# Spreading part of one weight matrix over few DMA engines and reordering the head and tail of a fused GQA-and-MLP decode kernel

## The chip, the cores and the metric

The kernel runs on one core of one Trainium2 chip. The metric is the device time of one execution in microseconds (us); the time before is the median of three runs, 681.97 us (681.95 to 682.03). A core has five engines (PE for matmuls, DVE for vector work, ACT for activations, POOL, and SP, which here only issues transfers) and sixteen DMA engines that bring data from main memory (HBM) into the on-chip memory (SBUF, 128 partitions).

## What is computed

One decode step of a block for 8 sequences: attention over a cache of 4096 positions (32 query heads that share 8 key/value heads in groups of 4), times a gate from a small gated MLP, plus the input.

```python
xn = _layernorm(x)                                  # 8 x 512
q  = xn @ wq                                        # 512 x 4096 weights
p  = softmax(q k^T * Dh**-0.5)                      # k_cache: 8 x 8 x 4096 x 128
s  = (p v) @ wo                                     # wo: 4096 x 512
z  = gelu(xn @ w_in);  z1, z2 = split(z);  z2 = _layernorm(z2)
g  = silu((z1 * (w_sp * z2 + b_sp)) @ w_out)        # w_out: 896 x 512
out = x + s * g
```

All data are 32-bit floats. The two caches are 134 MB each, so nearly all of the 291 MB that the kernel moves is read once and used once.

## The kernel before

**Loads.** Everything that comes from HBM goes through a ring of three SBUF slots of 16384 floats per partition (`ring`, `bufs=3`); a transfer into a slot is issued from SP's queue when the slot's last user is done. The order on SP is: one transfer `w_mlp` (L59: `w_in`, `w_out` and a small `side` block, 10880 floats per partition), `wq` (L74), and then for each of the 8 key/value heads two halves of K (`load_k`, L288) and two halves of V (`load_v`, L295). The input `x` (8 rows of 2 KB) is loaded from ACT's queue (L71). The last half of V comes in two pieces, with the output weights `wo` around it: blocks 0 to 7 ahead of it (L318) and blocks 8 to 31 behind it in nine pieces of falling size (`WO_PIECES`, L321), the last four of one block each (128 rows of 2 KB). A transfer over 128 partitions is shared by all sixteen DMA engines, eight rows each.

**Order of the work.** The head normalises `x` (L122 to L130), runs `mlp()` (L145 to L201, which leaves the gate in `gate`), then `project_q` twice (L208 to L220, which fills `qz`). Per head: `scores` for two halves (L231), `softmax` (L236 to L259), `values` for two halves (L273 to L278) and `combine` (L283). PE takes its instructions in the order in which the program writes them. Temporaries of `mlp()` lie in the unused end of the MLP's slot (`from_slot`), so that slot is free only when the last of them has been read.

**The tail.** The attention output of a head is split in 4 blocks of 128 rows, 32 blocks in all, and each has to be multiplied by its 128 x 512 block of `wo`. The first `FOLDED = 29` blocks go through `project_o` (L303): block `m` is accumulated over 512 columns in strip `m % 4` of PE (the array is used in four strips of 32 columns side by side) of the PSUM tile `part`. `part` is copied to SBUF by DVE (L342), and eight small matmuls (L358) add its four strips and two column halves into `acc`. The last three blocks go `direct` (L350): eight matmuls of 64 columns for each block put it straight into `acc`. The order on PE at the end is: blocks up to 28 folded, block 29 direct (`AHEAD = 30`), the eight matmuls of L358, blocks 30 and 31 direct, and then DVE multiplies by the gate (L362), adds `x` (L363), and ACT's queue stores (L364).

Of the kernel before, what the change touches and what calls it, by code (L numbers as in the profile page):

```python
# [8 lines left out]
F32 = mybir.dt.float32  # L9
# [4 lines left out]
P = 128  # L14
B, D = 8, 512
HKV, REP, S, DH = 8, 4, 4096, 128
NK = D // P
G = 4
J = S // (G * P)
R = 32  # L20
FH = 896
FQ = 256
NB = FH // P
EPS = 1e-5
GELU_C = 0.7978845608028654
HALF = B // 2
# [2 lines left out]
W = 64  # L29
OUT_ROWS = 2 * B  # L30
WO_EARLY = 8
WO_PIECES = [(8, 14), (14, 19), (19, 23), (23, 26), (26, 28), (28, 29), (29, 30), (30, 31), (31, 32)]
FOLDED = HKV * REP - 3
AHEAD = FOLDED + 1


@with_exitstack
def tile_gqa_gmlp_decode(ctx: ExitStack, tc: tile.TileContext, x, kT, v, wq, wo, w_mlp, out, gate, stored):
    nc = tc.nc
    head = ctx.enter_context(tc.tile_pool(name="head", bufs=1))  # L40
    l = head.tile([P, HKV], F32, name="l")
# [4 lines left out]
    const = ctx.enter_context(tc.tile_pool(name="const", bufs=1))  # L46
    work = ctx.enter_context(tc.tile_pool(name="work", bufs=1))
# [4 lines left out]
    def slot():  # L52
        return ring.tile([P, SLOT], F32, name="slot")


    mlp_slot = slot()
    n_in, n_out = NK * 2 * FH, NB * D
    n_mlp = n_in + n_out + P
    nc.sync.dma_start(mlp_slot[:, :n_mlp], w_mlp)  # L59
    w_in_sb = mlp_slot[:, :n_in].rearrange("p (k n) -> p k n", k=NK)  # L60
    w_out_sb = mlp_slot[:, n_in:n_in + n_out].rearrange("p (j d) -> p j d", j=NB)
    side_sb = mlp_slot[:, n_in + n_out:n_mlp]
    spare = [n_mlp]

    def from_slot(rows, n):
        lo = spare[0]
        spare[0] = lo + n
        return mlp_slot[:rows, lo:lo + n]

    x_sb = from_slot(B, D)  # L70
    nc.scalar.dma_start(x_sb, x)  # L71

    wq_sb = slot()
    nc.sync.dma_start(wq_sb, wq)  # L74
    wq_sb = wq_sb.rearrange("p (k n) -> p k n", k=NK)


    ident = const.tile([P, P], F32, name="ident")
# [44 lines left out]
    nc.vector.bn_aggr(mv, st)  # L123
    nc.vector.tensor_scalar(rstd[:, 0:1], mv[:, 1:2], EPS, None, op0=ALU.add)
    nc.gpsimd.tensor_tensor(rstd[:, 1:2], rstd[:, 0:1], neg_half[:B, 0:1], op=ALU.pow)
# [8 lines left out]
    def mlp():  # L134
        z = from_slot(P, 2 * FQ).rearrange("p (a f) -> p a f", a=2)
        u = from_slot(P, 2 * FQ).rearrange("p (a f) -> p a f", a=2)
        pz = scratch([P, 2 * FQ], "pz")
        nc.vector.memset(pz, 0.0)
        pz_v = pz.rearrange("p (a f) -> p a f", a=2)
        w_in_v = w_in_sb.rearrange("p k (a f) -> p k a f", a=2)  # L140
        for k in range(NK):
            for g in range(G):
                lo = g * FQ
                n = min(FQ, FH - lo)
                nc.tensor.matmul(pz_v[R * g:R * (g + 1), :, :n], xnT[:, k, :],  # L145
                                 w_in_v[:, k, :, lo:lo + n], start=(k == 0), stop=(k == NK - 1))
        zf, uf = z.rearrange("p a f -> p (a f)"), u.rearrange("p a f -> p (a f)")
        nc.vector.tensor_copy(zf, pz)
        nc.vector.tensor_mul(uf, zf, zf)
        nc.vector.tensor_scalar(uf, uf, 0.044715, 1.0, op0=ALU.mult, op1=ALU.add)  # L150
        nc.vector.tensor_mul(uf, uf, zf)
        nc.scalar.activation(uf, uf, AF.Tanh, scale=GELU_C)
        nc.vector.tensor_scalar(uf, uf, 1.0, 0.5, op0=ALU.add, op1=ALU.mult)
        nc.vector.tensor_mul(zf, uf, zf)

        def mean(src, name):
            part_sum = small.tile([P, 1], F32, name="part_sum")
            nc.vector.tensor_reduce(part_sum, src, op=ALU.add, axis=AX.X)  # L158
# [12 lines left out]
        nc.vector.tensor_scalar(var, var, EPS, None, op0=ALU.add)  # L171
        rs = small.tile([P, 1], F32, name="rs")
        nc.gpsimd.tensor_tensor(rs, var, neg_half, op=ALU.pow)
        nc.vector.tensor_scalar(z2, z2, rs, None, op0=ALU.mult)
        nc.vector.tensor_scalar(z2, z2, side_sb[:, W:W + 1], side_sb[:, W + 1:W + 2],
                                op0=ALU.mult, op1=ALU.add)
        nc.vector.tensor_mul(u[:, 1, :], z2, z1)
        hT = from_slot(P, 2 * P).rearrange("p (a s) -> p a s", a=2)
        for a in range(2):
            th = scratch([P, P], "th")  # L180
            nc.tensor.transpose(th, u[:, 1, a * P:(a + 1) * P], ident)
            nc.vector.tensor_copy(hT[:, a, :], th)  # L182
        pw = scratch([P, D], "pw")
        for j in range(NB):
            g, a = divmod(j, 2)
            nc.tensor.matmul(pw[R * g:R * (g + 1), :], hT[:, a, R * g:R * (g + 1)], w_out_sb[:, j, :],  # L186
                             start=(a == 0), stop=(a == 1 or j == NB - 1))
        y_sb = from_slot(P, D)
        nc.vector.tensor_copy(y_sb, pw)  # L189
        py = scratch([P, W], "py")  # L190
        for g in range(G):
            for a in range(2):
                nc.tensor.matmul(py[R * g:R * (g + 1), :], pick[:, a, :],
                                 y_sb[:, (2 * g + a) * W:(2 * g + a + 1) * W], start=(a == 0), stop=(a == 1))
        nc.vector.tensor_copy(x_out, side_sb[:, :W])
        e = from_slot(P, W)
        nc.vector.tensor_scalar(e, py, -1.0, 87.0, op0=ALU.mult, op1=ALU.min)
        nc.scalar.activation(e, e, AF.Exp)
        nc.vector.tensor_scalar(e, e, 1.0, None, op0=ALU.add)
        nc.vector.reciprocal(e, e)  # L200
        nc.vector.tensor_mul(gate, py, e)  # L201
# [17 lines left out]
                o = b * R + b * REP  # L219
                nc.vector.tensor_copy(qz[:, h, o:o + REP], tv[:, :, g, b])  # L220

    oT = const.tile([P, HKV, REP, B], F32, name="oT")
    oT_last = const.tile([P, REP, 2, OUT_ROWS], F32, name="oT_last")
    nc.gpsimd.memset(oT_last, 0.0)

# [72 lines left out]
    part = sc[:, 0, :]  # L298

    def project_o(lo, hi):  # L300
        for m in range(lo, hi):
            h, r = divmod(m, REP)
            nc.tensor.matmul(part[R * r:R * r + B, :], oT[:, h, r, :], wo_sb[:, m, :],  # L303
                             start=(m < REP), stop=(m >= FOLDED - REP))

    mlp()
    project_q(0)
    project_q(1)
    for h in range(HKV):
        for half in range(2):  # L310
            scores(h, half, load_k(h, half))
        pT = softmax(h)
        po = po_ps[:, h % 2]
        for half in range(2):
            last = h == HKV - 1 and half == 1
            if last:
                wo_slot = slot()
                nc.sync.dma_start(wo_slot[:, :WO_EARLY * D], wo[:, :WO_EARLY * D])  # L318
                v_sb = load_v(h, half, 2)
                for lo, hi in WO_PIECES:  # L320
                    nc.sync.dma_start(wo_slot[:, lo * D:hi * D], wo[:, lo * D:hi * D])  # L321
                wo_sb = wo_slot.rearrange("p (m d) -> p m d", d=D)
                project_o(0, WO_EARLY)
            else:
                v_sb = load_v(h, half, 1)
            n = 2 if last else HALF
            for i in range(0, HALF, n):
                done = values(half * HALF + i, n, pT, v_sb[:, i:i + n])
                if half or i:
                    combine(*o_prev, po)  # L330
                o_prev = done
        combine(*o_prev, po)
        po_t = po.rearrange("p (b r) -> p r b", r=REP)
        n = min(REP, FOLDED - h * REP)
        nc.vector.tensor_copy(oT[:, h, :n], po_t[:, :n])
        if n < REP:
            for a in range(2):
                nc.vector.tensor_copy(oT_last[:, n:, a, a * B:(a + 1) * B], po_t[:, n:])

    project_o(WO_EARLY, FOLDED)  # L340
    part_sb = work.tile([P, G, DH], F32, name="o_all")
# [11 lines left out]

    direct(FOLDED, AHEAD)
    for a in range(2):
        for g in range(G):
            c = (2 * g + a) * W
            nc.tensor.matmul(acc[R * g:R * g + OUT_ROWS, :], pick[:, a, :OUT_ROWS], part_f[:, c:c + W],  # L358
                             start=False, stop=False)
    direct(AHEAD, HKV * REP)  # L360

# [42 lines left out]
```

## Time and profile before

| what | value |
|---|---|
| median of 3 runs | 681.97 us (681.95 to 682.03) |
| the profiled execution's own time | 681.93 us |
| its span, first to last instruction | 680.4 us |
| DMA, mean rate over the span | 428 GB/s |
| PE busy / PE weight loads busy | 343.5 us (50%) / 91.9 us (14%) |
| DVE / ACT / POOL busy | 87.2 / 13.4 / 3.9 us |

The profile gives, for one execution, the busy time of each engine, the DMA engines' busy share, the chain of work that ended last, and groups of instructions with their source line. `L303` is line 303 of the kernel before; after the change the same statements stand at other lines.

### The profile page before, as it was taken

What the parts mean: (1) busy time and instruction counts of PE and PEld (TensorE: products, weight loads), DVE (VectorE), ACT (ScalarE), POOL (GpSimd) and SP (SyncE); (2) the same over time, 40 slices, a digit from 0 to 9 for tenths busy, and PEclk for the clock granted to TensorE, in tenths of its full rate; (3) what the DMA queues carried; (4) which work ended last, traced back from release to release, by engine and by line L of the source; (5) the groups of instructions that cost most, each with busy time, mean ns of one, the idle gap of its engine ahead of it and who ended that gap; (6) DMA issues with size and microseconds to landing.
All of it is one profiled execution on the core that took longest, in us unless ns stands there. A gap on an engine that the chain in (4) does not pass through costs nothing.

```text
span 680.4 us, 5199 instructions
## 1 busy us (share of the span) xinstructions
PE 343.5 (50%) x2380; PEld 91.9 (14%) x2380; DVE 87.2 (13%) x229; ACT 13.4 (2%) x27; POOL 3.9 (1%) x12
## 2 busy tenths in 40 slices
PE   0475544435555453455554444555553454555557
PEld 0121111111111110111111111111111111111111
DVE  2440011102110021102100021101101021101121
ACT  0000000000000000000000000000000000000000
POOL 1000000000000000000000000000000000000000
PEclk9786666788776667878765677787666678777689
DMA  9999999999999999999999999999999999999996
GB/s 390 432 433 432 432 432 432 432 432 443 436 439 436 439 432 429 432 432 432 432 432 432 432 439 429 443 432 432 429 432 429 432 447 432 439 432 435 417 420 273
DMA packets 6661, 291.15 MB, mean 428 GB/s; under 512 B 872, under 2 KB 872, under 8 KB 1648
## 3 DMA queue, kind: packets, MB, share of 16 engines
q1 hardware_dynamic: 6480, 290.79, 98.9%
q8 instruction: 18, 0.29, 0.2%
q10 hardware_dynamic: 160, 0.05, 0.0%
q14 instruction: 3, 0.02, 0.0%
HBM read 290.80 MB, written 0.03 MB: 427 GB/s over the span
## 4 chain that ended last, share of the span: by engine, by line
DMA 77%; PE 16%; issue 4%; another core or an unknown queue 2%; DVE 1%; POOL 0%; POOLq 0%
DMA slot<-in_v 43%; DMA slot<-in_kT 28%; PE sc L231 7%; PE o_ps L273 7%; DMA slot<-in_wo 6%; PE scr L208 1%; DMA slot<-in_x 0%; PE sc L303 0%; DVE q_sb L211 0%; PE scr L214 0%; DVE o_all L342 0%; DVE slot L189 0%; DVE st L122 0%; POOLq L398 0%
## 5 line engine op out<-in xcount | busy, mean ns | idle before, releaser
L231 PE MATMUL sc<-slot,qz 128*32 128x512 f32 x1024 | 148.9, 747 | 140.6 <-DMA slot<-in_kT 140.6
L273 PE MATMUL o_ps<-slot,pT 128*16 128x512 f32 x1024 | 149.5, 748 | 113.8 <-DMA slot<-in_v 113.8
L231 PEld LDWEIGHTS sc<-slot,qz 128*32 128x32 f32 x1024 | 38.4, 134 | 244.8 <-issue 158.8
L273 PEld LDWEIGHTS o_ps<-slot,pT 128*16 128x16 f32 x1024 | 33.3, 114 | 215.9 <-issue 154.1
L236 DVE TENSOR_REDUCE nm<-sc 128x1 f32<-128x1024 f32 x8 | 9.8, 1225 | 286.2 <-PE sc L231 286.2
L276 DVE TENSOR_TENSOR o_all<-o_ps,diag 128x512 f32<-128x512 f32 x17 | 11.8, 692 | 249.1 <-PE o_ps L273 249.1
L238 ACT ACTIVATE p<-sc,nm 128x1024 f32<-128x1024 f32 x8 | 8.9, 1113 | 577.9 <-DVE nm L236 577.9
L283 PE MATMUL po_ps<-fold,o_sb 128*128 128x16 f32 x30 | 6.3, 286 | 26.8 <-DVE o_sb L278 26.8
L278 DVE TENSOR_REDUCE o_sb<-o_all 128x128 f32<-128x512 f32 x17 | 17.8, 1047 | 0.6
L145 PE MATMUL scr<-slot,xnT 128*32 128x512 f32 (+1 forms) x32 | 5.8, 830 | 9.9 <-DMA slot<-in_w_mlp 9.9
L283 PEld LDWEIGHTS po_ps<-fold,o_sb 128*128 128x128 f32 x30 | 4.8, 199 | 40.6 <-DVE o_sb L278 40.6
L303 PE MATMUL sc<-slot,oT 128*8 128x512 f32 x58 | 9.5, 593 | 1.1 <-DMA slot<-in_wo 1.0
L259 DVE STREAM_TRANSPOSE pT<-p 128x1024 f32<-128x1024 f32 x8 | 10.0, 1246 | 0.3
L241 PE MATMUL scr<-ident,nm 128*1 128x128 f32 x8 | 2.2, 270 | 10.9 <-DVE nm L236 10.9
L208 PE MATMUL scr<-slot,xnT 128*32 128x512 f32 x64 | 7.3, 594 | 0.0
L254 PE MATMUL scr<-wl,same 128*128 128x1 f32 x16 | 3.2, 272 | 6.2 <-DVE wl L252 6.2
L257 DVE TENSOR_SCALAR p<-p,w 128x1024 f32<-128x1024 f32 x8 | 6.0, 753 | 0.3
L220 DVE COPY qz<-scr 128x4 f32<-128x4 f32 x64 | 4.6, 151 | 1.5 <-PE scr L214 1.5
L160 PE MATMUL scr<-part_sum,same 128*128 128x1 f32 x4 | 1.1, 348 | 7.0 <-DVE part_sum L158 7.0
L247 PE MATMUL scr<-ident,full 1*128 1x1 f32 x8 | 1.7, 215 | 5.1 <-DVE full L245 5.1
L186 PE MATMUL scr<-slot 128*32 128x512 f32 x14 | 3.9, 1061 | 0.2 <-DVE slot L182 0.2
L254 PEld LDWEIGHTS scr<-wl,same 128*128 128x128 f32 x16 | 2.8, 219 | 6.6 <-PE scr L247 6.6
(88 smaller groups left out, 55.9 us busy)
## 6 DMA issues: line engine op xcount, KB each, us to landing
slot<-in_v SPq DMA_DIRECT2D x2, 4096.0 KB, 30.4
slot<-in_w_mlp SPq DMA_DIRECT2D x1, 5440.0 KB, 15.5
slot<-in_wo SPq DMA_DIRECT2D x1, 2048.0 KB, 34.4
slot<-in_wo SPq DMA_DIRECT2D x1, 1536.0 KB, 38.2
slot<-in_wo SPq DMA_DIRECT2D x1, 1280.0 KB, 41.2
slot<-in_wo SPq DMA_DIRECT2D x1, 1024.0 KB, 43.1
slot<-in_wo SPq DMA_DIRECT2D x4, 256.0 KB, 18.9
slot<-in_wo SPq DMA_DIRECT2D x1, 768.0 KB
```

What stands on the lines that cost most here:

```text
L208: nc.tensor.matmul(pq[R * g:R * (g + 1), :], xnT[:, k, :], wq_sb[:, k, lo:lo + REP * DH], start=(k == 0), stop=(k == NK - 1))
L231: nc.tensor.matmul(sc[R * g:R * (g + 1), c, :], qz[:, h, b * R:(b + 1) * R], k_sb[:, i, c, g, :], start=(b == 0), stop=(b == B - 1))
L236: nc.vector.tensor_reduce(m, sc, op=ALU.max, axis=AX.XY, negate=True)
L238: nc.scalar.activation(p, sc.rearrange("p c s -> p (c s)"), AF.Exp, bias=m, accum_out=l[:, h:h + 1])
L254: nc.tensor.matmul(tot, same_all, wl, start=True, stop=True)
L257: nc.vector.tensor_scalar(p, p, w, None, op0=ALU.mult)
L259: nc.vector.transpose(pT.rearrange("p j b g r -> p j g b r"), p.rearrange("p (j g b r) -> p j g b r", j=J, g=G, b=B))
L273: nc.tensor.matmul(of[R * c:R * c + G * REP, :], pT[:, j, b0 + i], v_sb[:, i, j], start=(j < rows), stop=(j >= J - rows))
L276: nc.vector.tensor_mul(o_all, o, diag[:, :, None].to_broadcast([P, G, DH]))
L278: nc.vector.tensor_reduce(o_sb, o_all.rearrange("p g d -> p d g"), op=ALU.add, axis=AX.X)
L283: nc.tensor.matmul(po[:, b0 * REP:(b0 + n) * REP], o_sb, f.rearrange("p i r -> p (i r)"), start=True, stop=True)
L303: nc.tensor.matmul(part[R * r:R * r + B, :], oT[:, h, r, :], wo_sb[:, m, :], start=(m < REP), stop=(m >= FOLDED - REP))
```

## The change

- The head's loads are now all on SP's queue in the order `wq`, `x`, `w_mlp`, two new transfers, K; `project_q` runs ahead of `mlp()`.
- The last two of the seven 128-row blocks of `w_out` leave `w_mlp` (which shrinks from 10880 to 9856 floats per partition) and come by two transfers of their own: partitions 0 to 94 from an array of 5 groups of 19 rows, partitions 95 to 127 from an array of 3 groups of 11 rows, 4 KB a row. Each group of the source is followed by an unused row, so that the groups stay a dimension of their own.
- Two temporaries of `mlp()` (`y_sb`, `e`) move out of the MLP's slot into tiles of the pool `work`.
- `FOLDED` goes from 29 to 28, so that all of the last head goes direct; blocks 26 and 27 are folded in two halves of 256 columns, each half in a strip of its own. `AHEAD` stays 30, so blocks 28 and 29 go direct ahead of the eight matmuls that add up the strips.

```diff
+EXTRA = [(5, 19), (3, 11)]
+MOVED = 2
...
-FOLDED = HKV * REP - 3
-AHEAD = FOLDED + 1
+FOLDED = HKV * REP - REP
+AHEAD = FOLDED + 2
...
+    wq_sb = slot()
+    nc.sync.dma_start(wq_sb, wq)
     mlp_slot = slot()
...
-    nc.scalar.dma_start(x_sb, x)
-
-    wq_sb = slot()
-    nc.sync.dma_start(wq_sb, wq)
+    nc.sync.dma_start(x_sb, x)
+    nc.sync.dma_start(mlp_slot[:, :n_kept], w_mlp)
+    row = 0
+    for (k, n), src in zip(EXTRA, (w_ex0, w_ex1)):
+        nc.sync.dma_start(mlp_slot[row:row + k * n, n_kept:n_mlp], src[:, :n])
+        row += k * n
...
-        y_sb = from_slot(P, D)
+        y_sb = work.tile([P, 2 * D], F32, name="y_sb", tag="pT")[:, :D]
...
-        e = from_slot(P, W)
+        e = work.tile([P, W], F32, name="e", tag="o_all")
...
-            nc.tensor.matmul(part[R * r:R * r + B, :], oT[:, h, r, :], wo_sb[:, m, :],
-                             start=(m < REP), stop=(m >= FOLDED - REP))
-
-    mlp()
+            cuts = 2 if m >= FOLDED - 2 else 1
+            n = D // cuts
+            for i in range(cuts):
+                q = 2 * (r % 2) + i if cuts == 2 else r
+                nc.tensor.matmul(part[R * q:R * q + B, i * n:(i + 1) * n], oT[:, h, r, :],
+                                 wo_sb[:, m, i * n:(i + 1) * n], start=(m < REP), stop=(cuts == 2))
+
     project_q(0)
     project_q(1)
+    mlp()
...
+    row = 0
+    for i, (m, n) in enumerate(EXTRA):
+        e = np.zeros((m, n + 1, MOVED * D), np.float32)
+        e[:, :n] = w_out[row:row + m * n, (NB - MOVED) * D:].reshape(m, n, MOVED * D)
+        arrays[f"w_ex{i}"] = e
+        row += m * n
```

More of the change, by code (lines that the diff above doesn't have):

```diff
@@ L32, with tile_gqa_gmlp_decode @@
 WO_PIECES = [(8, 14), (14, 19), (19, 23), (23, 26), (26, 28), (28, 29), (29, 30), (30, 31), (31, 32)]
-FOLDED = HKV * REP - 3
-AHEAD = FOLDED + 1
+FOLDED = HKV * REP - REP
+AHEAD = FOLDED + 2
 @with_exitstack
-def tile_gqa_gmlp_decode(ctx: ExitStack, tc: tile.TileContext, x, kT, v, wq, wo, w_mlp, out, gate, stored):
+def tile_gqa_gmlp_decode(ctx: ExitStack, tc: tile.TileContext, x, kT, v, wq, wo, w_mlp, w_ex0, w_ex1, out, gate, stored):
     nc = tc.nc
@@ L53, in slot @@
         return ring.tile([P, SLOT], F32, name="slot")
+    wq_sb = slot()
+    nc.sync.dma_start(wq_sb, wq)
+    wq_sb = wq_sb.rearrange("p (k n) -> p k n", k=NK)
     mlp_slot = slot()
     n_in, n_out = NK * 2 * FH, NB * D
-    n_mlp = n_in + n_out + P
-    nc.sync.dma_start(mlp_slot[:, :n_mlp], w_mlp)
+    n_kept = n_in + P + n_out - MOVED * D
+    n_mlp = n_in + P + n_out
     w_in_sb = mlp_slot[:, :n_in].rearrange("p (k n) -> p k n", k=NK)
-    w_out_sb = mlp_slot[:, n_in:n_in + n_out].rearrange("p (j d) -> p j d", j=NB)
-    side_sb = mlp_slot[:, n_in + n_out:n_mlp]
+    side_sb = mlp_slot[:, n_in:n_in + P]
+    w_out_sb = mlp_slot[:, n_in + P:n_mlp].rearrange("p (j d) -> p j d", j=NB)
     spare = [n_mlp]
@@ L70, in tile_gqa_gmlp_decode @@
     x_sb = from_slot(B, D)
-    nc.scalar.dma_start(x_sb, x)
-    wq_sb = slot()
-    nc.sync.dma_start(wq_sb, wq)
-    wq_sb = wq_sb.rearrange("p (k n) -> p k n", k=NK)
+    nc.sync.dma_start(x_sb, x)
[4 more added lines that the diff above has]
+        row += k * n
     ident = const.tile([P, P], F32, name="ident")
@@ L220, in project_q @@
                 nc.vector.tensor_copy(qz[:, h, o:o + REP], tv[:, :, g, b])
-    oT = const.tile([P, HKV, REP, B], F32, name="oT")
+    oT = const.tile([P, HKV - 1, REP, B], F32, name="oT")
     oT_last = const.tile([P, REP, 2, OUT_ROWS], F32, name="oT_last")
@@ L333, in tile_gqa_gmlp_decode @@
         po_t = po.rearrange("p (b r) -> p r b", r=REP)
-        n = min(REP, FOLDED - h * REP)
-        nc.vector.tensor_copy(oT[:, h, :n], po_t[:, :n])
-        if n < REP:
+        if h < HKV - 1:
+            nc.vector.tensor_copy(oT[:, h], po_t)
+        else:
             for a in range(2):
-                nc.vector.tensor_copy(oT_last[:, n:, a, a * B:(a + 1) * B], po_t[:, n:])
+                nc.vector.tensor_copy(oT_last[:, :, a, a * B:(a + 1) * B], po_t)
     project_o(WO_EARLY, FOLDED)
@@ L380 @@
     vv = c(A_v_cache).reshape(2, HALF, HKV, P, J, G, DH)
+    w_out = c(B_w_out).reshape(NB, P, D).transpose(1, 0, 2).reshape(P, NB * D)
     arrays = {
@@ L388 @@
             c(B_w_in).reshape(NK, P, 2 * FH).transpose(1, 0, 2).reshape(P, NK * 2 * FH),
-            c(B_w_out).reshape(NB, P, D).transpose(1, 0, 2).reshape(P, NB * D),
-            side.reshape(P, P)], axis=1),
-    }
+            side.reshape(P, P), w_out[:, :(NB - MOVED) * D]], axis=1),
+    }
+    row = 0
[4 more added lines that the diff above has]
+        row += m * n
     nc = bacc.Bacc("TRN2", target_bir_lowering=False, num_devices=1, dynamic_dma_scratch_size=1024)
```

## The prediction

> **What bounds the kernel.** I read the page from the top: who is busy, then the DMA queues, then the chain at the end.
>
> ```profile
> span 680.4 us, 5199 instructions
> ...
> DMA  9999999999999999999999999999999999999996
> GB/s 390 432 433 432 432 432 432 432 432 443 436 439 436 439 432 429 432 432 432 432 432 432 432 439 429 443 432 432 429 432 429 432 447 432 439 432 435 417 420 273
> ...
> q1 hardware_dynamic: 6480, 290.79, 98.9%
> q8 instruction: 18, 0.29, 0.2%
> ...
> q14 instruction: 3, 0.02, 0.0%
> ```
>
> The sixteen DMA engines are busy in every slice but the last, at 432 GB/s, or 27 GB/s each. One queue carries the 290.8 MB of data; two others fetch instructions, 18 times 16 KB and three times 8 KB. No compute engine is near its limit, so only two things can shorten the run: the moment when the last DMA engine finishes, and what comes after it. The windows view over the last microseconds shows that the engines don't finish together (columns: stretch, its length, busy times, granted PE clock, then the share of the sixteen engines and GB/s).
>
> ```profile
> 670.50:672.50 2.00, 1.91 (x18) 0.21 (x10) 0.00 (x0) 0.00 (x0) 0.00 (x0) 1.00 1.01 406
> 672.70:673.10 0.40, 0.22 (x4) 0.00 (x0) 0.00 (x0) 0.00 (x0) 0.00 (x0) 1.00 0.75 297
> 673.10:673.40 0.30, 0.00 (x0) 0.00 (x0) 0.00 (x0) 0.00 (x0) 0.00 (x0) 1.00 0.65 253
> 673.50:674.40 0.90, 0.69 (x6) 0.11 (x6) 0.00 (x0) 0.00 (x0) 0.00 (x0) 1.00 0.59 232
> 674.60:675.60 1.00, 0.82 (x7) 0.10 (x4) 0.00 (x0) 0.00 (x0) 0.00 (x0) 1.00 0.53 203
> 676.10:676.70 0.60, 0.60 (x18) 0.35 (x16) 0.00 (x0) 0.00 (x0) 0.00 (x0) 1.00 0.13 51
> 676.85:677.05 0.20, 0.04 (x1) 0.00 (x0) 0.20 (x1) 0.00 (x0) 0.00 (x0) 1.00 0.08 31
> 677.15:677.40 0.25, 0.00 (x0) 0.00 (x0) 0.24 (x1) 0.00 (x0) 0.00 (x0) 1.00 0.00 0
> ```
>
> In sixteenths, the share goes from 16 to 9 (0.59) around 673.1, to 8 (0.53) near 674.5, to 2 (0.13) near 675.9, to 1 (0.08) near 676.8, and to nothing by about 677.1. So seven engines are done at 672.8 to 673.4 and the last one 4.0 later. The steps are about 1.4 apart, which fits the instruction fetches. The view of the DMA queues in a 1.1 us window around one of them:
>
> ```profile
> q8 instruction: 1, 0.02, 5.5%
> ```
>
> That is 5.5% of 16 x 1.1, so 0.97 us of one engine, and the data packet behind it has to catch up. Eighteen fetches dealt in turn to eight engines give six of them two (2.8 late) and two of them three (4.2 late); the three small ones on a single engine account for the step near 674.5. That is the staircase, and I take it as the explanation. The kernel ends with its slowest engine, while seven lie idle for up to four microseconds.
>
> The chain of waits in its last stretch (start, us, what):
>
> ```profile
> 637.33 37.56 DMA slot<-in_wo
> 674.88 0.04 issue
> 674.92 1.76 PE sc L303 x6
> 676.68 0.02 issue
> 676.70 0.70 DVE o_all L342
> 677.41 0.04 issue
> 677.45 0.42 PE acc L358 x16
> 677.87 0.49 PE acc L350 x32
> 678.36 0.02 issue
> 678.38 0.24 DVE gate L362
> ```
>
> Blocks 26 and 27 land at 674.88. The four pieces behind them are 16 KB an engine each, 0.61 us at 27 GB/s, so the last lands at 674.88 + 4 x 0.61 = 677.3 (call it Z); the gate multiply starts 1.06 after Z. The chain doesn't run through that last landing: it runs through block 28 (folded), the DVE copy, and L358.
>
> **The change, part by part.**
>
> *DMA balance.* Two blocks leave `w_mlp`: eight rows of 4 KB on each engine. A row takes 4096 B / 27 GB/s = 0.152, so every engine is relieved of 1.2. The new transfers give their engines 19 rows (2.9) and 11 rows (1.7). I read them as running on five and on three engines, the three among the five: three engines get 4.55, two get 2.9. If these five are among the seven early ones, the engine ends become: three-fetch engine 677.1 - 1.2 = 675.9; the two engines 673.4 - 1.2 + 2.9 = 675.1; the three engines, from 672.8 to 673.4, 676.15 to 676.75. The last end moves from 677.1 to the upper part of that, I take 676.5: **0.6 gained** (0.35 to 0.95).
>
> [...] No view here names a packet's engine.
>
> [...]
>
> *Order of the head.* The rows of the timeline:
>
> ```profile
> 1.63 39.10 SPq L288 DMA_DIRECT2D slot<-in_kT  x2
> 3.21 0.68 DVE L122 BATCH_NORM_STATS2 st<-slot 8x6 f32<-8x512 f32 x1 [1.07 <-DMA slot<-in_x]
> 6.43 0.19 DVE L130 COPY xnT<-scr 128x32 f32<-128x32 f32 x1
> 16.33 5.81 PE L145 MATMUL scr<-slot,xnT 128*32 128x512 f32 x32 [9.94 <-DMA slot<-in_w_mlp]
> 38.44 3.64 PE L208 MATMUL scr<-slot,xnT 128*32 128x512 f32 x32
> 40.10 0.22 DVE L201 TENSOR_TENSOR gate<-scr,slot 128x64 f32<-128x64 f32 x1
> 47.91 0.66 PE L214 MATMUL scr<-ident,q_sb 128*128 128x128 f32 x4 [0.81 <-DVE q_sb L211]
> 55.84 9.97 PE L231 MATMUL sc<-slot,qz 128*32 128x512 f32 x64 [7.27 <-DMA slot<-in_kT]
> 75.04 5.48 PE L231 MATMUL sc<-slot,qz 128*32 128x512 f32 x32 [9.23 <-DMA slot<-in_kT]
> ```
>
> `wq` is 8.4 MB where `w_mlp` was 5.6; 2.8 MB more at 432 GB/s puts its landing, and `x` behind it, at about 16.3 + 6.5 = 22.8. Normalising takes 3.4 (3.21 to 6.62): 26.2. The two q projections hold PE for 10.1 (38.44 to 48.57): 36.3. `w_mlp` has landed by then (22.8 + 11.7 = 34.5), and the two moved blocks, at worst 4.6 later, are wanted only at the end of the MLP. The MLP takes 24.0 (16.33 to 40.32), so it ends at about 60. The first scores start near 59 to 60 and not at 55.84, and end near 70; the second half of K still lands at about 75, where PE had waited 9.23. The delay of 4 disappears in that wait.
>
> On SP the second K waits for the `wq` slot (about 36), the first V for the MLP's slot (about 60), and behind it the second V for the first scores (about 70). The DMA engines by then hold the second K up to about 75 and the first V up to 94: they don't run dry, with 15 us of cover. Moving `y_sb` and `e` out of the slot only frees it sooner. **Cost nothing**; with the cover gone, each microsecond that SP is late would cost one. `x` on SP's queue is one issue of about 0.4 more, ahead of 19 us of queued data.
>
> *Tail.* Three rows of the groups and the timeline:
>
> ```profile
> L303 PE MATMUL sc<-slot,oT 128*8 128x512 f32 x58 | 9.5, 593 | 1.1 <-DMA slot<-in_wo 1.0
> ...
> L350 PE MATMUL acc<-slot,oT_last 128*16 128x64 f32 x48 | 1.3, 220 | 0.0
> ...
> 673.71 1.04 PE L303 MATMUL sc<-slot,oT 128*8 128x512 f32 x6 [0.79 <-DMA slot<-in_wo]
> ```
>
> Each matmul of the program is two PE instructions. Three blocks in three strips took 1.04, as one does: strips run side by side, the second pass 1.04 - 0.59 = 0.43 behind the first. For 256 columns I interpolate between 593 ns (512 columns) and 220 ns (64): 380 ns, second pass 0.22 behind, so four halves in four strips take 0.6. In times before Z: blocks 26 and 27 land at Z - 2.44, are folded at Z - 1.8 and copied (0.70) at Z - 1.1. Blocks 28 and 29, the latter landed at Z - 1.22, go direct by about Z - 0.9. L358 takes 0.42 to Z - 0.5, block 30 follows by Z - 0.25, and PE is free when block 31 lands. Its eight matmuls cost what the eight of L358 did, 0.42, plus 0.04 ahead and 0.07 to DVE: the gate multiply starts at Z + 0.53 instead of Z + 1.06. **0.5 gained.** If the halves ran one after the other (8 x 0.22 + 0.16 = 1.9), the copy would end at Z + 0.2 and nearly all of this gain would go; the three strips above speak against it, so the bounds are 0.1 and 0.55. All later steps (two DVE operations, store) stay.
>
> *Instructions.* One more folded matmul and eight more direct ones are 36 PE instructions and their weight loads together, a seventh of what one fetch covers (4760 by 18). A nineteenth fetch could put 1.4 on one engine; it matters only on one with three fetches (675.9 + 1.4 = 677.3, which takes the 0.6 back). Value nothing.
>
> **Sum.** 0.6 + 0.5 = 1.1 off the profiled execution's 681.93 gives 680.83. The median is 0.04 above that execution: 680.87, so **680.9 us**, with a range of its own of 680.4 to 681.5 (gains of 1.55 and 0.45).
>
> **Rivals.**
>
> *The first engines aren't all early.* An engine with three added groups ends 3.35 later than before. If one of the three has the small fetches, the end is 674.5 + 3.35 = 677.85, 0.75 late less 0.5: 682.2. If one has two or three fetches: 679.25 or 680.45, less 0.5: 683.6 or 684.8, slower. [...]
>
> *Writes to partitions that another engine is filling.* This is my case for the other side. All other transfers give an engine eight rows of its own share; the new ones give it rows that lie in the shares of others. If the partitions of a share take in no more than the 27 GB/s that one engine brings, then a row that meets a busy neighbour takes twice as long, and the neighbour loses the 1.2 that it was to gain. If 11 of 16 rows meet one (eleven engines stream on), 30 rows cost 11/16 x 4.55 = 3.1 more: 680.9 + 3.1 = 684.0; with all of them, 685.4. It decides from 1.1 / 30 = 0.037 per row, a quarter more than 0.152. The place is 34 to 42 us into the run, where `w_mlp` ends on those engines. Nothing in the profile of before shows two engines writing into one share for long, so it speaks neither way.
>
> [...]
>
> *The split doesn't happen.* If the new transfers spread over all sixteen engines, the 1.2 taken off is put back, and only the tail remains: 681.5.
>
> **Chances.** Forecast 0.64; split doesn't happen 0.04; first engines not early 0.17 (0.06 of it the mild 682.2); partition writes 0.15, of which a third is a weaker form below 683.3. A measurement of this kernel can tell about 0.2%, 1.36 us, from no change: the limits are 680.6 and 683.3. About a quarter of the forecast's chance lies below 680.6. Faster 0.16, within 0.63, slower 0.21. The range goes from 680.4, the forecast's lower end, to 684.0, the partition case at 11 of 16; beyond it lie the three-fetch case, the harder half of the partition case and a little below, less than 2 in 10.
>
> **What would show it.** Balance: in the windows view of the last microseconds the share should hold near 16/16 longer and fall within some 2 to 3 us instead of 4, with two to four engines early. If the last engine ends later than 677.1, a rival is right. Partition writes: packets near 34 to 42 us longer, and the first K later than 59. Head: no slice of the DMA row below 9. Tail: the direct matmuls of block 31 waiting for a DMA, and the gate multiply some 0.5 after the last landing. Wrong altogether if scores wait for the MLP beyond 75 us, or the DMA row shows a gap there.

## The result and the profile after

The changed kernel takes 684.16 us (median of 10; 683.87 to 684.61) beside 682.10 for the kernel before in the same comparison: a ratio of 1.0029, with a 95% interval of 1.0021 to 1.0038. It is 2 us slower, where 1.1 us faster was forecast.

The page of the kernel after, the lines that answer to those shown of before (span, DMA share and rate in 40 slices, the queues):

```profile
span 682.6 us, 5238 instructions
...
DMA  9999999999999999999999999999999999999997
GB/s 399 436 337 450 438 439 427 430 427 430 431 426 446 435 434 431 430 443 434 431 438 435 426 434 432 430 439 438 427 430 427 430 446 431 434 443 449 397 422 300
...
q1 hardware_dynamic: 6632, 290.80, 99.1%
q8 instruction: 19, 0.31, 0.2%
```

The busy share says that nothing happened: every slice has a 9 until the last. The rate under it says where the time went. The third slice, 34 to 51 us, moved 337 GB/s where the same slice before moved 433: 96 GB/s x 17 us is 1.6 MB, or 3.8 us of all sixteen engines. A DMA engine counts as busy while its packet is slow (the third slice has its 9 at 337 GB/s as at 433), so share and rate have to be read together. The view books a packet where it starts, 64 KB at a time on each engine, so the edges of such a stretch can shift by up to 1 MB; what was lost is read more closely from the packets and landings below.

The windows view over the last microseconds of after (stretch, length, busy times, PE clock, share of the engines, GB/s):

```profile
672.50:674.20 1.70, 1.49 (x11) 0.53 (x14) 0.77 (x3) 0.00 (x0) 0.00 (x0) 1.00 1.00 411
675.30:676.90 1.60, 1.60 (x10) 0.11 (x6) 0.00 (x0) 0.00 (x0) 0.00 (x0) 1.00 0.85 334
677.80:678.80 1.00, 0.77 (x40) 0.55 (x40) 0.69 (x1) 0.00 (x0) 0.00 (x0) 1.00 0.40 154
679.20:679.40 0.20, 0.20 (x16) 0.20 (x16) 0.00 (x0) 0.00 (x0) 0.00 (x0) 1.00 0.30 113
679.55:679.80 0.25, 0.03 (x4) 0.00 (x0) 0.00 (x0) 0.00 (x0) 0.00 (x0) 1.00 0.00 0
```

Three engines stop between 674.2 and 675.3, most of the rest before 677.8, and five run on (0.30 of sixteen) until about 679.5. The staircase is still some 5 us long, and all of it has moved back, the early engines too: without any loss they would have stopped 1.2 sooner than the 672.8 to 673.4 of before.

The place of the loss, by the same view for 34 to 46 us, before and then after:

```profile
34.00:46.00 12.00, 10.39 (x90) 3.29 (x86) 4.87 (x38) 0.26 (x1) 0.00 (x0) 0.84 1.02 439
```

```profile
34.00:46.00 12.00, 7.81 (x68) 2.50 (x65) 8.34 (x71) 0.62 (x1) 0.00 (x0) 0.98 0.85 284
```

And the DMA view of after in the two microseconds from 35 to 37, where five engines bring the 4 KB rows (in the trace's records eleven 64 KB packets of K start between 33.4 and 33.9, which leaves five of sixteen):

```profile
DMA packets 39, 0.16 MB, mean 80 GB/s; under 512 B 0, under 2 KB 0, under 8 KB 39
q1 hardware_dynamic: 39, 0.16, 32.5%
```

In 2 us five engines started 39 rows: 5 x 2 / 39 = 0.256 us a row, not 0.152. The share says nearly the same: 32.5% of 16 x 2 us, divided by 39, is 0.267. From 38.5 to 40.5, when only three engines should have rows left (two more packets of K start at 37.9 and 38.0), it is 24 rows, 0.25 us each:

```profile
DMA packets 24, 0.10 MB, mean 49 GB/s; under 512 B 0, under 2 KB 0, under 8 KB 24
```

The trace records when each packet started and how long it took, though no view prints them one by one. The rows that started before 33.8 us took 0.159 each, those that started from 34.0 on took 0.22 to 0.32. None of the latter was spared, although the first group's rows go to partitions 0 to 18, which are the five engines' own by the layout that e1's expectation assumes. The eleven engines that were loading K were slowed as well: their first 64 KB packet took 3.70 to 4.01 and their second 4.11 to 4.23, where 2.42 is the median before. That is some 3 us lost on every one of them.

The timeline of after, the first scores and the tail:

```profile
61.40 9.31 PE L237 MATMUL sc<-slot,qz 128*32 128x512 f32 x64 [2.00 <-DMA slot<-in_kT]
80.60 9.94 PE L237 MATMUL sc<-slot,qz 128*32 128x512 f32 x64 [9.90 <-DMA slot<-in_kT]
...
677.25 0.62 PE L313 MATMUL sc<-slot,oT 128*8 128x256 f32 x8 [0.22 <-DMA slot<-in_wo]
677.94 0.69 DVE L352 COPY o_all<-sc 128x512 f32<-128x512 f32 x1 [4.18 <-PE sc L313]
677.99 0.95 PE L360 MATMUL acc<-slot,oT_last 128*16 128x64 f32 x32
678.76 0.41 PE L368 MATMUL acc<-o_all,pick 128*16 128x64 f32 x16
679.16 0.42 PE L360 MATMUL acc<-slot,oT_last 128*16 128x64 f32 x16
679.80 0.42 PE L360 MATMUL acc<-slot,oT_last 128*16 128x64 f32 x16 [0.22 <-DMA slot<-in_wo]
680.29 0.23 DVE L372 TENSOR_TENSOR gate<-acc,gate 128x64 f32<-128x64 f32 x1 [1.66 <-PE acc L360]
```

The tail does what was forecast: PE is free when the last block lands, the four halves take 0.62 side by side, and the gate multiply starts 0.53 after the landing, which the chain of waits puts at 668.63 + 11.13 = 679.76:

```profile
668.63 11.13 DMA slot<-in_wo
679.76 0.04 issue
```

So the run is late by the DMA engines alone: the last landing came 2.4 later than the 677.3 of before, less 0.5 in the tail.

### The profile page after: what moved, and what is told of

It reads as the page before. It is cut to its first block, busy times and chain, and to the rows that moved or that the text cites. A ratio compares the mean times of both kernels' runs of the same rounds, so it can differ in the third digit from the quotient of the medians.

```text
span 682.6 us, 5238 instructions
## 1 busy us (share of the span) xinstructions
PE 339.4 (50%) x2398; PEld 91.3 (13%) x2398; DVE 87.4 (13%) x228; ACT 13.4 (2%) x27; POOL 3.9 (1%) x12
## 4 chain that ended last, share of the span: by engine, by line
DMA 81%; PE 13%; issue 4%; another core or an unknown queue 1%; DVE 0%; SPq 0%; POOLq 0%; POOL 0%
DMA slot<-in_kT 36%; DMA slot<-in_v 35%; DMA slot<-in_wo 7%; PE sc L237 7%; PE o_ps L279 7%; DMA slot<-in_x 3%; SPq L301 0%; DVE st L128 0%; POOLq L414 0%; POOL rstd L131 0%; DVE slot L188 0%; PE scr L187 0%; PE acc L360 0%; DVE slot L183 0%
## 5 line engine op out<-in xcount | busy, mean ns | idle before, releaser
L237 PE MATMUL sc<-slot,qz 128*32 128x512 f32 x1024 | 146.5, 737 | 138.6 <-DMA slot<-in_kT 138.6
L279 PE MATMUL o_ps<-slot,pT 128*16 128x512 f32 x1024 | 147.2, 739 | 113.3 <-DMA slot<-in_v 113.3
L214 PE MATMUL scr<-slot,xnT 128*32 128x512 f32 x64 | 10.2, 794 | 0.3 <-DVE xnT L136 0.3
L313 PE MATMUL sc<-slot,oT 128*8 128x512 f32 (+1 forms) x60 | 8.1, 564 | 0.2 <-DMA slot<-in_wo 0.2
```

Source lines behind the costliest of these rows:

```text
L214: nc.tensor.matmul(pq[R * g:R * (g + 1), :], xnT[:, k, :], wq_sb[:, k, lo:lo + REP * DH], start=(k == 0), stop=(k == NK - 1))
L237: nc.tensor.matmul(sc[R * g:R * (g + 1), c, :], qz[:, h, b * R:(b + 1) * R], k_sb[:, i, c, g, :], start=(b == 0), stop=(b == B - 1))
L279: nc.tensor.matmul(of[R * c:R * c + G * REP, :], pT[:, j, b0 + i], v_sb[:, i, j], start=(j < rows), stop=(j >= J - rows))
L313: nc.tensor.matmul(part[R * q:R * q + B, i * n:(i + 1) * n], oT[:, h, r, :], wo_sb[:, m, i * n:(i + 1) * n], start=(m < REP), stop=(cuts = ...
```

## The experiments

Theory A is the rival of the prediction: a row written into a share of partitions that another engine is filling is slow, and slows others. Against it stand B (the new transfers are slow in themselves: few engines, small rows, their source), C (the first five engines aren't early), and D (the new order of the head costs something). Times in a comparison are medians beside the kernel before on the same chip (682.16, 682.13 and 682.17 in the three comparisons). No view names the engine of a packet or the partitions that it fills. Which partitions are an engine's own share is an assumption, stated in e1's expectation; eight rows for each engine don't show it. The runs fit it: e1 and e2, with the same bytes, are 4.75 us apart. Shares, and engines counted as first to seventh, are by this layout in all that follows.

**e1_own_share and e2_far_share: the same bytes, other partitions.**

```diff
-EXTRA = [(5, 19), (3, 11)]
+EXTRA = [(5, 2432), (3, 1408)]
+BASE = 0          # e2: BASE = 64
...
-        nc.sync.dma_start(mlp_slot[row:row + k * n, n_kept:n_mlp], src[:, :n])
+        lo -= n
+        for i in range(2):
+            nc.sync.dma_start(mlp_slot[BASE + R * i:BASE + R * i + 4 * k, lo:lo + n], src[:, 5 * i:5 * i + 4])
```

> The changed kernel, but the bytes of the two new transfers go elsewhere: five groups of four rows to partitions 0-19 and 32-51, three groups of four rows to partitions 0-11 and 32-43, 9.7 and 5.6 KB a row, so the same 78 KB and 45 KB per engine, into free room of the same slot. If partition p is written by engine (p/4 modulo 8) in an ordinary transfer, as equal shares of eight rows suggest, each engine now writes only partitions of its own share. The w_out blocks 5 and 6 are left out (blocks 3 and 4 are used in their place). Theory A (a row that meets a partition share which another engine is filling takes about twice as long, and slows that engine): no slow rows, the first K lands near 58 instead of 61.3, and the time is the recorded forecast, 1.0 below the kernel before (0.7 to 1.4 below). Theory B (the new transfers are slow in themselves: few engines, their source, or their small rows): as the changed kernel, 2 above the kernel before. Theory C (the first engines are among the late ones): 1.5 or more above the kernel before, without slow rows at 34 to 42 us.

> As e1_own_share, with 64 added to each destination partition and nothing else changed: the same engines, sources, row sizes and bytes, into shares that five other engines are filling with K. The w_out blocks 5 and 6 are left out as there. Theory A: every row meets a busy neighbour, 30 rows' worth at half speed is 4.5 more than e1, so 3.5 above the kernel before, and 4.5 above e1; DMA rate well under 430 GB/s in the windows from 34 to 43 us. Theory B: the same time as e1, both 2 above the kernel before. Theory C: the same as e1.

Measured: e1 680.80, ratio 0.9979 (0.9970 to 0.9988), 1.4 below the kernel before. e2 685.55, ratio 1.0047 (1.0034 to 1.0059), 3.4 above it and 4.75 above e1. The windows view of e1 in the disputed stretch and at the end, and the first scores:

```profile
34.00:46.00 12.00, 7.61 (x68) 2.46 (x60) 8.30 (x71) 0.63 (x1) 0.00 (x0) 0.96 1.03 443
...
671.30:671.60 0.30, 0.30 (x9) 0.00 (x0) 0.00 (x0) 0.00 (x0) 0.00 (x0) 1.00 1.19 492
671.90:672.30 0.40, 0.26 (x4) 0.00 (x0) 0.00 (x0) 0.00 (x0) 0.00 (x0) 1.00 0.82 328
```

```profile
58.96 8.57 PE L239 MATMUL sc<-slot,qz 128*32 128x512 f32 x64
```

The same of e2:

```profile
34.00:46.00 12.00, 7.71 (x68) 2.46 (x60) 8.30 (x72) 0.63 (x1) 0.00 (x0) 0.97 0.91 274
...
676.20:676.50 0.30, 0.30 (x8) 0.00 (x0) 0.00 (x0) 0.00 (x0) 0.00 (x0) 1.00 0.94 389
677.00:678.00 1.00, 0.46 (x6) 0.11 (x6) 0.00 (x0) 0.00 (x0) 0.00 (x0) 1.00 0.83 328
```

```profile
62.70 7.71 PE L239 MATMUL sc<-slot,qz 128*32 128x512 f32 x56 [3.39 <-DMA slot<-in_kT]
```

The two kernels differ in the number of the destination partition and in nothing else, so few engines and their source cost nothing in themselves. Small rows don't either, though e1's are larger: in e3, below, all 128 rows of 4 KB took 0.159 us, and so did the first rows of the change. Theory B is out, and so is C, since e1's five engines took the same bytes and the run got faster. Theory A gave the 4.5 between them. It was too small in one respect: three engines stop by 672.3 in e1 and only near 676.5 in e2, some 4 later. The rate over 34 to 46 us fell by 169 GB/s x 12 us = 2.0 MB; rows at half speed account for 3 x 4.5 + 2 x 2.9 = 19 engine-microseconds, 0.5 MB, and the five engines whose shares are written would lose another 0.5. About half of the loss seems to lie elsewhere (the edges of the stretch leave that open), and the DMA view of e2 from 33.9 to 37.7 us shows that it does:

```profile
DMA packets 35, 0.29 MB, mean 77 GB/s; under 512 B 5, under 2 KB 5, under 8 KB 5
```

Thirty rows of 9.7 KB are all of the 0.29 MB (the other five packets are tiny). So none of the eleven engines that load K finished its 64 KB packet and began another in 3.8 us, where such a packet takes 64 KB / 27 GB/s = 2.4. In the trace's records their first packet took 4.25 to 4.65 and their second 4.81 to 4.98, all eleven alike. By the layout only five of the eleven fill shares that e2 writes to: the other six are slowed as well.

**e3_one_transfer and e4_tail_alone: the change without its few-engine transfers, and the tail alone.**

```diff
-    for (k, n), src in zip(EXTRA, (w_ex0, w_ex1)):
-        nc.sync.dma_start(mlp_slot[row:row + k * n, n_kept:n_mlp], src[:, :n])
-        row += k * n
+    nc.sync.dma_start(mlp_slot[:, n_kept:n_mlp], w_ex)      # e3; w_ex is 128 x 1024
```

e4 is the kernel before with `FOLDED = HKV * REP - REP`, `AHEAD = FOLDED + 2` and the new `project_o`.

> The changed kernel, but the two moved w_out blocks come by one transfer over 128 partitions, so over all sixteen engines, eight rows of 4 KB each. Order of the head and tail as in the change. Theory A and C: no engine gets more than before, rows take 0.15 us; the DMA ends where it did before the change and only the tail's gain is left: 0.5 below the kernel before (0.3 to 0.7). If the new order of the head costs something of its own (theory D), it stays at or above the kernel before, up to 2 above.

> The kernel before with only the new fold: 28 blocks folded, blocks 26 and 27 in halves, four blocks direct. Loads and order of the head as before. All theories on the DMA: 0.5 below the kernel before (0.1 if the halves run one after the other); the last direct matmuls wait for the landing of the last block, and the gate multiply starts about 0.5 after it instead of 1.0.

Measured: 681.79 for both, ratios 0.9992 (0.9983 to 1.0001) and 0.9993 (0.9985 to 1.0002): 0.4 below the kernel before, at the edge of what these runs can tell from nothing. The order of the head costs nothing that shows (D, which allowed up to 2 us, is out at that size), and the tail's gain is near the 0.5. The chain of waits and then the timeline of e4:

```profile
666.31 11.56 DMA slot<-in_wo
677.87 0.04 issue
```

```profile
677.91 0.42 PE L354 MATMUL acc<-slot,oT_last 128*16 128x64 f32 x16 [0.22 <-DMA slot<-in_wo]
678.40 0.22 DVE L366 TENSOR_TENSOR gate<-acc,gate 128x64 f32<-128x64 f32 x1 [1.61 <-PE acc L354]
```

Here too the gate multiply starts 0.53 after the last landing, where the kernel before took 1.06 by the prediction's sum and 1.00 from the last landing in its trace, at 677.38. In this profiled execution the landing itself was half a microsecond later than in the profile of before.

**e6_next_share and e7_part_far: how far does the slowing reach?** Both leave w_out blocks 5 and 6 out. e6 is e1 with `BASE = 4`; e7 is e1 with 64 added for the three-group transfers alone.

```diff
-BASE = 0
+BASE = {5: 0, 3: 64}      # e7
```

> As e1_own_share (w_out blocks 5 and 6 left out), with 4 added to each destination partition: each of the five engines now writes the share of the engine after it. Four of these five shares get nothing else at that time, since their own engines are busy with the new rows; only the fifth engine's rows (partitions 20-23 and 52-55) meet an engine that is loading K. Theory A-local (a row is slow only if its share is being filled, and slows only the engine that fills it): the three engines with both groups stay at full speed, the fifth engine ends 2.9 later, near 678: 1.3 above e1_own_share, about the time of the kernel before, and the first scores start as in e1. Theory A-wide (rows outside an engine's own share slow all engines, whatever they fill): as e2_far_share, 3 above the kernel before.

> As e1_own_share, with 64 added only to the destinations of the three-group transfers; the five-group transfers stay on their own shares (w_out blocks 5 and 6 left out). Bytes outside own shares: 45 KB on each of three engines, 135 KB, where e2_far_share has 525 KB. Theory A-local: 1.7 of rows at half speed, 1.7 above e1_own_share, and the engines whose shares aren't written end as in e1. Theory A-wide, by time: e2's three engines with no rows of their own and no rows written into their shares ended 4.4 later than in e1; the rows here last a third as long (1.7 of 4.5), so 1.6 for those engines, and 1.6 to 1.8 above e1 for the end. The two differ in the early engines: 0 against 1.6 later than in e1.

Measured: e7 682.47 (ratio 1.0003, 0.9994 to 1.0012), 1.7 above e1, which both forms of A expected; e6 683.12 (1.0012, 1.0004 to 1.0021), 2.3 above e1, between local (1.3) and wide (over 4). The first scores, which wait for the slowest engine's K, and the share at 671.30 to 673.20 in e7:

```profile
59.74 8.77 PE L239 MATMUL sc<-slot,qz 128*32 128x512 f32 x64 [1.65 <-DMA slot<-in_kT]
```

```profile
671.30:673.20 1.90, 1.90 (x20) 0.38 (x12) 0.01 (x1) 0.00 (x0) 0.00 (x0) 1.00 0.99 407
674.00:675.00 1.00, 0.61 (x6) 0.11 (x6) 0.00 (x0) 0.00 (x0) 0.00 (x0) 1.00 0.84 332
```

In e7 the three early engines, done by 672.3 in e1, work until 673.2 and beyond, as the share of 0.99 says. The table has the 64 KB packets of K on the engines that were loading it, and when the last transfer's sixteen parts landed; both are read from the trace's own records, in microseconds.

| run | first K packet | second K packet | the three earliest landings | the last |
|---|---|---|---|---|
| e1 | 2.42 | 2.42 to 2.44 | 672.0, 672.0, 672.3 | 676.6 |
| e7 | 2.42 | 3.39 to 3.86 | 673.3, 673.6, 673.7 | 678.2 |
| e6 | 2.66 to 2.72, one 5.04 | 3.82 to 3.83 | 673.5, 673.5, 673.9 | 678.7 |
| after | 3.70 to 4.01 | 4.11 to 4.23 | 675.1, 675.2, 675.4 | 679.8 |
| e2 | 4.25 to 4.65 | 4.81 to 4.98 | 676.4, 676.5, 676.7 | 681.3 |

So the early engines of e7 end 1.3 to 1.6 later than in e1, against 0 (local) and 1.6 (wide) expected: about a third of what e2 took from them (4.4), with rows outside their own shares for about a third of the time. That speaks for the wide form.

e6 seems to lie between the two forms because its expectation overlooked a collision. The fourth engine has only the larger rows and finishes them at 36.9 us. It then loads K into its own share, to which the third engine, by the layout, is still writing. Up to there one K packet, on the share that the fifth engine's rows go to, takes 5.04, and the other ten are only a tenth slower than in e1. The next packet of those ten, under way when this second collision began, takes 3.8. The rows whose targets nobody else fills cost little at first (0.41 instead of 0.37), then twice their time (0.44 instead of 0.22). One collision slows engines that have no part in it, and how much differs from case to case. What exactly is shared between the engines stays open.

**e5_half_rows: all of the first eight engines.** The whole computation, the two blocks in halves of 64 rows on partitions 0 to 63.

```diff
+    for i in range(2):
+        nc.sync.dma_start(mlp_slot[R * i:R * (i + 1), n_kept:n_mlp], w_ex[i, :, :4])
...
+                for c, t in enumerate((hT[:KH], hT2)):
+                    nc.tensor.matmul(pw[R * g:R * (g + 1), :], t[:, a, R * g:R * (g + 1)],
+                                     w_half_sb[:, c, j - NB + MOVED, :], start=first and c == 0, stop=final and c == 1)
```

> The whole computation, with the moved w_out blocks 5 and 6 laid out as halves of 64 rows on partitions 0-63 alone: two transfers of 32 partitions over eight engines each (partitions 0-31, then 32-63), so that every engine of the first eight writes its own share, 64 KB each, and the other eight get nothing. Two more small transposes and four matmuls over 64 rows in place of two over 128, ahead of the first scores. Rest as in the change. Theory A: all engines are relieved of 1.2, the first eight get 2.4: the three-fetch engines end at 675.9 and bound the run, the first eight at 674.6, one of them with the small fetches at 675.7. That is 1.2 from the DMA engines and 0.5 from the tail (of which e4 showed 0.4): 1.6 below the kernel before (1.2 to 1.8), and 0.3 below e1_own_share. If the first eight hold late engines (theory C), 1 or more above the kernel before. If rows written by few engines slow the others wherever they go, 1 to 2 above the kernel before.

Measured: 681.53, ratio 0.9996 (0.9987 to 1.0005), 0.6 below the kernel before and not 1.6: a miss. Its runs fall into two groups, 681.3 to 681.7 and 682.6 to 682.9; the profile is one of the second. Its last microseconds:

```profile
672.20:673.70 1.50, 1.50 (x14) 0.63 (x18) 0.29 (x2) 0.00 (x0) 0.00 (x0) 1.00 0.91 356
675.80:676.60 0.80, 0.80 (x11) 0.12 (x8) 0.00 (x0) 0.00 (x0) 0.00 (x0) 1.00 0.13 51
677.70:678.20 0.50, 0.50 (x34) 0.30 (x21) 0.00 (x0) 0.00 (x0) 0.00 (x0) 1.00 0.06 25
```

One engine alone runs on for over a microsecond. In the trace's records the last two landings are at 677.4 and 678.5, where the expectation had 675.9 for the last. That fits two engines with added rows and with 16 KB fetches on top, two fetches on one and three on the other (676.1 and 677.4 in the landings of before, plus the 1.2 that such an engine has more). So the first eight hold late engines; e9 and e10 ask where they begin.

**e9_six_own and e10_seven_own: which engines are early.** e1 with `EXTRA = [(6, 3840)]` or `[(7, 3840)]`, w_out blocks 5 and 6 left out.

> As e1_own_share, but one group of transfers over six engines, 123 KB on each, all on their own shares (partitions 0-23 and 32-55); w_out blocks 5 and 6 left out. Each of the six ends 3.3 later than before the change (4.5 added, 1.2 taken). Five early engines and one more early one: the engine with the small fetches, if among them, bounds at 674.5 + 3.3 = 677.8, else the early ones at 676.7: 0.3 above the kernel before, or 0.8 below. If the sixth engine takes 16 KB fetches: 675.85 + 3.3 = 679.2 or more, so 1.7 or more above the kernel before.

> As e9_six_own over seven engines (partitions 0-27 and 32-59), 123 KB on each; w_out blocks 5 and 6 left out. e5_half_rows ended 1.1 later than expected, which fits late engines among the first eight. If the seventh engine is early, the time is that of e9_six_own. If it takes 16 KB fetches, it ends at 679.2 with two or 680.4 with three: 1.7 to 2.9 above the kernel before, and 1.4 or more above e9_six_own unless the sixth is late already.

Measured: e9 683.92 (ratio 1.0026, 1.0017 to 1.0036), 1.75 above the kernel before; e10 683.70 (1.0024, 1.0015 to 1.0034). The sixth engine is late, and a seventh adds nothing to the time. The windows view of e10, then of e9; e9's profile is of its longest run, 685.26:

```profile
672.50:674.20 1.70, 1.50 (x11) 0.60 (x14) 0.80 (x3) 0.00 (x0) 0.00 (x0) 1.00 0.83 329
```

```profile
672.50:674.20 1.70, 1.70 (x11) 0.38 (x10) 0.15 (x2) 0.00 (x0) 0.00 (x0) 1.00 0.83 328
...
676.50:678.00 1.50, 0.78 (x6) 0.11 (x6) 0.00 (x0) 0.00 (x0) 0.00 (x0) 1.00 0.15 59
678.00:679.50 1.50, 1.21 (x27) 0.39 (x24) 0.37 (x1) 0.00 (x0) 0.00 (x0) 1.00 0.06 25
679.50:680.50 1.00, 0.89 (x51) 0.64 (x48) 0.33 (x1) 0.00 (x0) 0.00 (x0) 1.00 0.07 27
```

In both, three of sixteen engines are idle by then, as in e1: these early ones are not among the seven that got added bytes. In e9 a single engine runs on from 678.0 to 680.5, at 25 to 27 GB/s, so it wasn't slowed, only late. In the landings of the last transfer e10 has two such engines, at 679.3 and 679.6, where e9 has one, at 680.9. That fits a seventh engine that is late as well, and a sixth that took three fetches in e9's profile and two in e10's.

**e8_real_five: a version that computes everything.** One w_out block moves, in four pieces on partitions 0 to 19 and 32 to 51, with zero weights between.

```diff
+MOVED = 1
+KP = 52
+PIECES = [(0, 0, 32), (20, 20, 52), (72, 72, 104), (92, 92, 124)]
...
+    for i in range(2):
+        nc.sync.dma_start(mlp_slot[R * i:R * i + 20, n_kept:n_mlp], w_ex[i, :, :4])
...
+                for c in range(len(PIECES)):
+                    nc.tensor.matmul(pw[R * g:R * (g + 1), :], hTp[:, c, R * g:R * (g + 1)], w_piece_sb[:, c, :],
+                                     start=(c == 0), stop=(c == len(PIECES) - 1))
```

> The whole computation, with one w_out block (the last) moved. Its 128 rows stand in four pieces on partitions 0-19 and 32-51, the shares of the first five engines, with zero weights in the gap and for rows that a piece would repeat: two transfers over five engines, 65 KB each, all on their own shares. Four small transposes and four matmuls over 52 rows take the place of one over 128, ahead of the first scores. Order of the head and the tail as in the change. Theory A with the first five free of the 16 KB fetches: all engines are relieved of 0.6, the five get 2.4; the three-fetch engines end at 676.5, the engine with the small fetches, if it is among the five, at 676.3, the other four near 675: 0.6 from the DMA engines and 0.4 from the tail, 1.0 below the kernel before (0.6 to 1.2), below e3_one_transfer and e4_tail_alone. If the first five weren't early, or if few engines' rows were slow anywhere, above e3_one_transfer.

Measured: 681.03, ratio 0.9980 (0.9972 to 0.9989): 1.1 below the kernel before, 0.8 below e3 and e4, 3.1 below the change. Its windows, chain and timeline:

```profile
670.00:672.00 2.00, 2.00 (x20) 0.40 (x12) 0.08 (x1) 0.00 (x0) 0.00 (x0) 1.00 1.01 416
673.50:674.90 1.40, 1.21 (x14) 0.12 (x8) 0.00 (x0) 0.00 (x0) 0.00 (x0) 1.00 0.83 320
675.70:676.40 0.70, 0.70 (x44) 0.53 (x46) 0.00 (x0) 0.00 (x0) 0.00 (x0) 1.00 0.17 64
676.50:676.80 0.30, 0.15 (x12) 0.00 (x0) 0.00 (x0) 0.00 (x0) 0.00 (x0) 1.00 0.00 0
```

```profile
665.75 11.07 DMA slot<-in_wo
676.83 0.04 issue
```

```profile
677.35 0.23 DVE L383 TENSOR_TENSOR gate<-acc,gate 128x64 f32<-128x64 f32 x1 [1.66 <-PE acc L371]
```

The last engines end at about 676.5, the 676.5 of its sum. The staircase as a whole is as long as before (the first landing of the last transfer is at 672.5 and the last at 676.8, before 673.1 and 677.4), since three early engines still get nothing added; all of it has moved forward by 0.6.

## Why the prediction was wrong, point by point

- **The step that failed** is the first term, "A row takes 4096 B / 27 GB/s = 0.152". It is about right for a row in an engine's own share (0.159 in e3) and was used for rows in the shares of others, where the run shows 0.25. With it went the unstated premise that the engines loading K are left alone: each of them lost 3 us. Thirty rows are then 7.5 and not 4.55, the three engines end at 676.5 + 3.0 = 679.5, and 679.5 is where the share drops to zero. The "0.6 gained" became 2.4 lost.
- **The explanation of the staircase** held. The last transfer's landings in the trace of before are seven at 673.1 to 673.7, one at 674.8, six at 676.1 to 676.3, and then 677.0 and 677.4, as its steps have them. Removing 1.2 from all engines and adding up to 4.55 to the first five gave 1.4 in e1, tail included, and e8 ended where its sum said.
- **"If these five are among the seven early ones"**: right in effect. The first five take the added bytes and the run still gains (e1, e8), and with the sixth it loses (e9). One of the five seems to be the engine with the small fetches: in e9 the last landing but one is at 678.2, where the expectation had 677.8 for that engine. The rival with a chance of 0.17 was wrong. That the new transfers run on five engines and on three of these five was assumed, and no view of before shows it. What after shows fits: eleven packets of K start when the rows do, and the number of rows started in 2 us falls from 39 to 24, by about 5 to 3, once the groups of 19 rows are done. Which five they are no run names; the sixth engine of e9 differs from the first five.
- **The head**: "Cost nothing" held (e3 and e4 both 681.79). The MLP ended a microsecond later than forecast, but with a wait of 9.90 for the next K behind it; in after the first scores waited 2.00 for K, in e1 not at all.
- **The tail**: the mechanism and its 0.53 held; the gain was 0.47 counted from the last landing (1.00 less 0.53), and the time it gave 0.4 of the 0.5, with an interval that touches no change.
- **The fetches**: a nineteenth came in after and also in e1 and e8, which were faster; it could not decide the end, since in all three traces it starts after the last packet of data (in after at 680.26, 0.8 later).
- **The rival that came true** was the writes to partitions that another engine is filling, priced at 684.0 with 11 of 16 rows slow; measured were 684.16. Its price for the writing engines came out (3.1 forecast, 3.0 measured), in part by luck: it had 11 of 16 rows at twice their time, and in the run nearly all rows took some 1.6 times theirs. Its price for the neighbours was wrong: it gave 1.2 to those whose share is written, and engines lost 3 in after and 4.4 in e2, there whether their share was written to or not. It had 0.15 because the profile of before shows no two engines writing into one share for long, and that was too little. Its premise, that a share takes in no more than the 27 GB/s of one engine, no run shows by itself. Moving rows by 64 partitions cost 4.75 (e2 beside e1), which fits it, but the six engines of e2 that by the layout fill other partitions lost as much as the five that meet the rows (second packets of 4.81 to 4.98 on all eleven), so a limit of each share isn't the whole.
- **The range**: the bounds 0.95 and 0.55 add up to 1.50 and not 1.55, so its lower end should have been 680.5; nothing hangs on it.

## What to carry to other kernels

When DMA engines bound a kernel, look at when each of them stops, not only at the mean share, and even them out. But a DMA engine's load isn't free to move: rows that go to partitions which another engine is filling took 1.6 to 1.7 times as long here (0.25 us instead of 0.159 in after; 5 x 3.8 / 30 = 0.63 in e2, where such a row undisturbed took 0.37), and they held up every engine that was loading (64 KB packets of 3.70 to 4.98 us in after and e2, where 2.42 is the median before). So extra bytes for an idle engine have to be laid out on that engine's own partitions, even at the price of zeros and a few small matmuls (e8: 681.03 beside 684.16). When a resource is busy by the profile, compare its rate with the same stretch of another run: a slowed transfer counted as busy here (a 9 at 337 GB/s).

## What the runs showed of the hardware that wasn't expected

- Rows written into busy shares slowed all engines that were loading at the time, six of them in e2 by the layout on neither side of the collision: the earliest three ended 3.1 (after) and 4.4 us (e2) later than in e1, and the mean rate over 34 to 46 us fell from 443 to 284 and 274 GB/s. What the engines share there, no run here shows.
- The late engines seem to be the same ones from run to run: e1, e8, e9 and e10 fit the first five free of the 16 KB fetches, the sixth not, and three outside the first seven free again. Each of the eighteen fetches of before took 0.88 to 0.96 us, in which its engine moved no data (fifteen packets of data are under way in the middle of sixteen of the fetches, fourteen in that of the two that overlap a small fetch), and where a 64 KB packet came next it took 2.89 to 2.97 instead of 2.42: 1.4 us together, the height of a step. The fetches' times repeat after every eighth (0.96, 0.96, 0.95, 0.88, 0.88, 0.94, 0.93 and 0.93, then the same within 0.01), which fits eight engines served in turn. So the lateness fits the fetches in size and number; no run took them away.
